# Moving a tenth of the first layer's exponentials from ScalarE to VectorE in a two-attention kernel, with the exponential's bias given as a number

## The chip, the cores and the metric

One core of one Trainium2 chip. The metric is the device time of one launch in microseconds (us). A run is called fast unless it lies over 1.5% above the fastest of the same kernel; only fast runs enter ratios. "Clock" is the mean clock that TensorE was granted over the run, 1.0 being full speed. The engines' names in the profile: DVE is VectorE, POOL is GpSimd, ACT is ScalarE, PE is TensorE.

## The reference, cut to what matters

Two attention layers on separate inputs, 2048 tokens, 32 heads of 16 channels, outputs side by side. The first sees all keys, the second only the last 256.

```python
def _A_ref(x, wqkv, wo):                       # D = 512, H = 32, Dh = 16
    q, k, v = split(x @ wqkv)
    scores = jnp.einsum("bhqd,bhkd->bhqk", q, k) * (Dh ** -0.5)
    p = softmax(scores)
    return (p @ v) @ wo
# _B_ref: the same, with scores masked to 0 <= query - key < 256
# result: concatenate([_A_ref(...), _B_ref(...)], axis=-1)
```

Almost all work is the exponential: 2048 x 2048 x 32 for the first layer, some 12% of that for the second.

## The kernel before

A **job** is one head, 128 keys and 512 queries. Four jobs (four heads) make a group, sixteen groups a unit of the first layer; there are 32 such units, and 32 short ones of the windowed layer strewn between them. Three jobs share a **slot**: a score tile of three PSUM banks, of which there are two, and one exponential over 3 x 512 columns.

```python
def scores(self, slot):                        # TensorE, two slots ahead
    sps = self.ps.tile([P, SLOT, 512], FP32, name="sps", tag="sps", bufs=2)
    for b, jb in enumerate(slot["jobs"]):
        r = slice(32 * jb.j, 32 * jb.j + KR)   # 32 of the 128 rows
        if b == 0 and self.filled < 2:         # "idle fill": a 128-row product,
            self.nc.tensor.matmul(sps[:, 0, 0:WARM], ...)   # overwritten at once
        ...
        self.nc.tensor.matmul(sps[:, b, ...], lhsT=kT[r, ...], rhs=qT[r, ...], ...)

def exps(self, slot):                          # ScalarE
    nc.scalar.activation(out=pT[:, b:e, :n], in_=sps[:, b:e, :n], func=ACT.Exp, scale=SCALE)
    ...                                        # masks of the windowed layer:
    # diagonal blocks: product with a 0/1 tile on VectorE; the others: a select on GpSimd

def values(self, upto):                        # TensorE, into the one bank "op"
    ...                                        # four products of 32 columns, side by side
```

The program's PSUM tiles are six banks of scores, one bank "op" for values, one bank "ms" for all else (projections, and so on), which VectorE empties. The projections and the output products go in between as `steps`, at most one or two a slot; `self.filled` counts those of the slot before. In each loop TensorE gets: the scores of two slots ahead, the values of an earlier slot, then the steps.

## Time and profile before

| | before |
|---|---|
| time | 1166.54 us at the prediction; 1167.79 with the run beside the change |
| ScalarE busy | 1098.6 us, 94% |
| VectorE, GpSimd busy | 298.2 and 119.0 us |
| TensorE clock | 0.939 |
| full exponentials (1536 columns) | 782, one every 1.33 us when nothing is waited for |

The prediction below shows the lines. In a line of a group, the first numbers are busy time and the mean length of one instruction; then come the engine's idle time just before them and what ended it. The row of tenths named PEclk, one figure per fortieth of the span, is near 9 almost throughout, and falls to 6 and 7 near the end, where the kernel has few steps to place.

### The profile page before, as it was taken

The numbers are of one execution on the slowest core, as the hardware profiler recorded it, in microseconds if no ns is written. First come the engines' busy times: TensorE is split into PE (matmuls) and PEld (weight loads), VectorE is DVE, ScalarE is ACT, GpSimd is POOL, SyncE is SP. The second block draws the span as 40 slices with busy tenths as digits, with TensorE's granted clock in tenths as the row PEclk, the third lists the DMA queues.
The fourth block names the chain that finished last, engine by engine and source line by source line (L and its number), as shares of the span: only waits on it lengthen the run. The fifth ranks groups of instructions, "written<-read, shape, count | busy, mean of one in ns | idle before, by whom it ended". The sixth has DMA issues, their size and how long they took to land.

```text
span 1169.9 us, 17451 instructions
## 1 busy us (share of the span) xinstructions
PE 926.1 (79%) x6844; PEld 270.6 (23%) x6944; DVE 298.2 (25%) x674; ACT 1098.6 (94%) x841; POOL 119.0 (10%) x316
## 2 busy tenths in 40 slices
PE   6788888878878887777778787787777887788893
PEld 3222222222222222222222222222222222222221
DVE  3442121132123222222322232224223132320101
ACT  3789999998999999999999999999999999999992
POOL 4000000010001001011200121102112011210100
PEclk9999899998999898999999999999999999976777
DMA  6022421221222112211220221124012112210101
GB/s 207 10 77 75 99 83 41 61 63 52 65 78 76 45 42 65 70 47 61 83 66 32 75 76 54 39 68 118 26 48 65 65 65 69 66 43 18 57 19 55
DMA packets 72810, 73.87 MB, mean 63 GB/s; under 512 B 22688, under 2 KB 55832, under 8 KB 72728
## 3 DMA queue, kind: packets, MB, share of 16 engines
q1 hardware_dynamic: 69656, 68.83, 19.3%
q10 hardware_dynamic: 2432, 1.84, 0.5%
q0 software_dynamic: 640, 2.10, 0.5%
q8 instruction: 54, 0.88, 0.3%
q14 instruction: 28, 0.23, 0.1%
HBM read 39.06 MB, written 31.58 MB: 60 GB/s over the span
## 4 chain that ended last, share of the span: by engine, by line
ACT 62%; PE 21%; issue 11%; DVE 3%; DMA 1%; POOL 0%; ACTq 0%; another core or an unknown queue 0%; SPq 0%; DVEq 0%; POOLq 0%
ACT pT L480 61%; PE sps L462 6%; PE sps L457 6%; PE ms L202 4%; PE op L514 4%; DVE va L285 1%; DVE osb L533 1%; PE ms L591 0%; DMA den<-od 0%; DVE pT L491 0%; DMA rb<-rd 0%; PE sps L358 0%; ACT xT L610 0%; DVE padmax L394 0%; DVE kTa L392 0%
## 5 line engine op out<-in xcount | busy, mean ns | idle before, releaser
L480 ACT ACTIVATE pT<-sps 128x1536 bf16<-128x1536 f32 (+4 forms) x827 | 1088.4, 1566 | 32.8 <-PE sps L462 31.1
L457 PE MATMUL sps<-qTa,kTa 128*128 128x512 bf16 x659 | 261.0, 396 | 159.2 <-ACT pT L480 152.9
L462 PE MATMUL sps<-qTa,kTa 32*128 32x512 bf16 x2048 | 286.5, 404 | 1.5 <-ACT pT L480 1.5
L514 PE MATMUL op<-pT,va 128*32 128x512 bf16 x2048 | 216.4, 412 | 0.5 <-DVE osb L533 0.3
L493 POOL TENSOR_SCALAR_AFFINE_SELECT pT<-pT 128x256 bf16<-128x256 bf16 (+2 forms) x224 | 102.5, 475 | 967.7 <-issue 556.6
L462 PEld LDWEIGHTS <-kTa 32*128 32x128 bf16 x2048 | 68.2, 91 | 395.3 <-issue 395.3
L491 DVE TENSOR_TENSOR pT<-pT,mlo 128x256 bf16<-128x256 bf16 (+2 forms) x256 | 74.9, 334 | 136.3 <-ACT pT L480 134.9
L457 PEld LDWEIGHTS <-kTa 128*128 128x128 bf16 x659 | 64.3, 98 | 144.4 <-issue 124.4
L514 PEld LDWEIGHTS <-va 128*32 128x32 bf16 x2048 | 53.7, 94 | 125.5 <-issue 125.0
L457 PE MATMUL sps<-qTb,kTb 128*128 128x512 bf16 x128 | 51.2, 400 | 34.8 <-ACT pT L480 32.7
L533 DVE COPY osb<-op 128x512 f32<-128x512 f32 x64 | 44.2, 691 | 85.2 <-PE op L514 84.9
L462 PE MATMUL sps<-qTb,kTb 32*128 32x384 bf16 (+2 forms) x704 | 58.4, 289 | 0.0
L220 DVE CAST kst<-ms 128x512 bf16<-128x512 f32 x28 | 19.4, 691 | 141.4 <-PE ms L202 141.4
L343 DVE CAST ob<-ms 128x512 bf16<-128x512 f32 x28 | 19.4, 691 | 131.8 <-PE ms L202 131.8
L301 DVE CAST qs<-ms 128x512 bf16<-128x512 f32 x31 | 21.4, 690 | 115.1 <-PE ms L202 115.1
L514 PE MATMUL op<-pT,vb 128*32 128x384 bf16 (+2 forms) x704 | 36.6, 290 | 0.9 <-DVE osb L533 0.7
L202 PE MATMUL ms<-xT,wq 128*128 128x512 bf16 x91 | 32.2, 408 | 4.7 <-issue 4.3
L462 PEld LDWEIGHTS <-kTb 32*128 32x128 bf16 x704 | 16.9, 93 | 79.7 <-issue 79.7
L202 PE MATMUL ms<-wv,xT 128*128 128x512 bf16 x103 | 32.0, 398 | 4.2 <-issue 1.6
L202 PE MATMUL ms<-xT,wk 128*128 128x512 bf16 x89 | 30.9, 413 | 3.5 <-issue 2.7
L285 DVE CAST vb<-ms 128x512 bf16<-128x512 f32 x16 | 11.1, 692 | 84.5 <-PE ms L202 84.5
L312 DVE CAST gs<-ms 8x512 bf16<-8x512 f32 x31 | 21.0, 677 | 20.0 <-PE ms L310 20.0
(80 smaller groups left out, 274.8 us busy)
## 6 DMA issues: line engine op xcount, KB each, us to landing
od<-osb SPq DMA_DIRECT2D x64, 256.0 KB
oc<-od SPq DMA_DIRECT2D x32, 256.0 KB
rb<-rd SPq DMA_DIRECT2D x32, 256.0 KB
kTb<-kd SPq DMA_DIRECT2D x16, 256.0 KB
qTb<-qd SPq DMA_DIRECT2D x16, 256.0 KB
qd<-qs SPq DMA_DIRECT2D x31, 128.0 KB
qTa<-qd SPq DMA_DIRECT2D x15, 256.0 KB
out_dram<-ob SPq DMA_DIRECT2D x30, 128.0 KB
```

The source lines that it names most:

```text
L202: self.nc.tensor.matmul(bank, lhsT=lhs(c), rhs=rhs(c), start=(c == 0), stop=(c == NC - 1))
L220: copy(out=kst[:], in_=bank)
L285: copy(out=v3[:, :, 1:VP], in_=bank.rearrange("p (h d) -> p h d", d=DH))
L301: copy(out=qs[:], in_=bank)
L312: self.nc.vector.tensor_copy(out=gs[:], in_=b[0:8, :])
L457: self.nc.tensor.matmul(sps[:, 0, 0:WARM], lhsT=kT[:, gg, k0:k0 + P], rhs=qT[:, gg, 0:WARM], start=True, stop=True)
L462: self.nc.tensor.matmul(sps[:, b, o:o + q1 - q0], lhsT=kT[r, gg, k0:k0 + P], rhs=qT[r, gg, q0:q1], start=True, stop=True, tile_position=(3 ...
L480: nc.scalar.activation(out=pT[:, b:e, :n], in_=sps[:, b:e, :n], func=ACT.Exp, scale=SCALE)
L491: nc.vector.tensor_mul(out=v, in0=v, in1=self.mlo[:, 0:e - b, :])
L493: nc.gpsimd.affine_select(v, v, pattern=[[0, e - b], [-1, P]], compare_op=ALU.is_ge, fill=0.0, base=-1, channel_multiplier=1)
L514: self.nc.tensor.matmul(op[32 * jb.j:32 * jb.j + 32, q0:q1], lhsT=self.v[jb.inst, kt][:, h * VP:h * VP + 32], rhs=slot["pT"][:, b, o:o + q ...
L533: nc.vector.tensor_copy(out=osb[:], in_=self.op[i, p, g][:])
```

## The change

Intent: ScalarE is busy for 94% of the span and VectorE for 25%, so VectorE takes a tenth of the first layer's exponentials (196 of 2048 jobs). The scores of a moved job are scaled so that their fp32 value, written as a 16-bit whole number, has the bits of a bf16 power of two; a cubic in the low half corrects it. To have one kind of scores for both engines, the queries are scaled by log2(e) and 128 and carry an offset, which ScalarE takes off with a bias. Masks leave VectorE, and several buffers shrink to make room. The diff is cut: masked values are also used one slot later, and the start-up has other filler products; e1_no_moved, below, keeps all of it but the moved jobs.

```diff
-QRING = (3, 4)
-KRING_B = 10
-VRING_B = 12
+QRING = (3, 3)
+KRING_B = 8
+VRING_B = 10
+FIRST_D = 4                # units 0 to 3 move nothing
+PACE_D = (2, 2, 2, 1)      # groups moved per unit, in turn
 # exps
             nc.scalar.activation(out=pT[:, b:e, :n], in_=sps[:, b:e, :n], func=ACT.Exp,
-                                 scale=SCALE)
+                                 scale=LN2 / 128, bias=-127 * LN2)
-                if kind == "d":
-                    nc.vector.tensor_mul(out=v, in0=v, in1=self.mlo[:, 0:e - b, :])
-                else:
-                    nc.gpsimd.affine_select(...)
+                nc.gpsimd.affine_select(...)          # both kinds
 # new: one step per moved job
+    def poly_ok(self, key):
+        return key[:2] + (key[2] // 2,) in self.qT and len(self.dq) < 4
+    def poly_steps(self, group):
+        def step(jb):
+            b = self.bank()                           # the one bank "ms"
+            nc.tensor.matmul(b[:], lhsT=kT[r, ...], rhs=..., ...)
+            nc.vector.tensor_copy(out=y[:, half, :], in_=b[:])
+            if half == 0:
+                return
+            # first, second: dh = f(low 16 bits of y); third: pD = dh * c + y
+            # each a scalar_tensor_tensor on 128 x 1024
+            self.dq += [first, second, third]
 # end of each slot
+            for _ in range(min(2, len(self.dq))):
+                self.dq.pop(0)()
```

## The prediction

> **What bounds the kernel now.** I read, in this order, the busy shares, the chain of waits, the groups by shape, and the timeline of one steady stretch. The busy shares name the engine:

> ```profile
> PE 926.1 (79%) x6844; PEld 270.6 (23%) x6944; DVE 298.2 (25%) x674; ACT 1098.6 (94%) x841; POOL 119.0 (10%) x316
> ...
> PEclk9999899998999898999999999999999999976777
> ```
> ScalarE is busy for 94% of the span; VectorE and GpSimd for 25% and 10%; the granted TensorE clock (PEclk, tenths) is near full until the last eighth. Whoever takes exponentials away from ScalarE shortens the span, as long as something else does not become the pace. The chain of waits, by engine, agrees:

> ```profile
> ACT 62%; PE 21%; issue 11%; DVE 3%; DMA 1%; POOL 0%; ACTq 0%; another core or an unknown queue 0%; SPq 0%; DVEq 0%; POOLq 0%
> ```
> ScalarE carries most of it; the TensorE part is the hand-over of scores, since PSUM holds two score tiles of three banks. The groups by shape (busy us, mean ns, then idle time before them) give the sizes:

> ```profile
> L480 ACT ACTIVATE pT<-sps 128x1536 bf16<-128x1536 f32 x782 | 1058.6, 1608 | 30.4 <-PE sps L462 28.9 <-DVE pT L491 1.0
> ...
> L457 PE MATMUL sps<-qTa,kTa 128*128 128x512 bf16 x659 | 261.0, 396 | 159.2 <-ACT pT L480 152.9
> ...
> L533 DVE COPY osb<-op 128x512 f32<-128x512 f32 x64 | 44.2, 691 | 85.2 <-PE op L514 84.9
> L493 POOL TENSOR_SCALAR_AFFINE_SELECT pT<-pT 128x384 bf16<-128x384 bf16 x70 | 43.2, 625 | 265.7 <-issue 177.9 <-ACT pT L480 79.7 <-POOL pT L493 4.4
> ...
> L493 POOL TENSOR_SCALAR_AFFINE_SELECT pT<-pT 128x256 bf16<-128x256 bf16 x84 | 38.2, 468 | 455.2 <-ACT pT L480 271.6 <-issue 178.2 <-POOL pT L493 4.6
> ...
> L491 DVE TENSOR_TENSOR pT<-pT,mlo 128x384 bf16<-128x384 bf16 x86 | 30.9, 381 | 77.1 <-ACT pT L480 76.3 <-POOL pT L493 0.7
> ...
> L493 POOL TENSOR_SCALAR_AFFINE_SELECT pT<-pT 128x128 bf16<-128x128 bf16 x70 | 22.9, 334 | 246.8 <-issue 200.5 <-ACT pT L480 40.4 <-POOL pT L493 4.7
> ...
> L559 DVE TENSOR_TENSOR oTb<-oc,rb 128x512 bf16<-128x512 f32 x16 | 11.0, 685 | 21.0 <-DMA rb<-rd 21.0
> ```
> Of the exponentials 782 are full slots (three jobs of 512 columns); they waited only 30.4 us in all. The 659 products of L457 are extra products that the program puts in when little other work was placed; they are idle fill, so TensorE's 79% overstates it. The mean of 1608 ns contains time queued behind the one before, so the price of a slot comes from the timeline, five in a row:

> ```profile
> start us, us, engine line op out<-in xcount [idle before <-releaser]
> 599.72 6.83 ACT L480 ACTIVATE pT<-sps 128x1536 bf16<-128x1536 f32 x5
> ```
> Five end 6.83 us after the first starts. With the last one's own length of about 1.5 us left out, four starts take 5.33 us: **1.33 us a slot**. (Busy time over count, 1058.6/782, gives 1.35 with small waits in it.) By the same timeline TensorE places one idle-fill product, three scores and four value products in about 0.96 us of such a slot: it can be late by a few tenths of a us plus the one buffered slot before ScalarE notices, about 1.3 us in all.

> [...]
> - [...] The first eight full exponentials of this trace, before a queue forms, have a mean of 1459 ns (the groups of the stretch from 26 to 40 us). [...] the built instructions of both kernels show a plain number there. That part of the title buys nothing by itself; it only undoes the offset in the new scores.
> - [...] the trace's 128x512 fp32 product (L559, shown above) has a mean of 685. [...]
> - [...] the 128x384 selects have a mean of 625 ns, while single ones with no two-input VectorE work beside them have 516 to 520 (read instruction by instruction).

> **The change part by part.**
> 1. *Removed from ScalarE.* 28 of the 32 units of the full attention give up 2, 2, 2, 1 of their 16 key groups in turn: 49 groups of 4 jobs, 196 jobs of 2432. The new program's instruction order has 716 full exponentials in place of 782, with two or three more of the small shapes. 66 x 1.33 = 87.8 us, less about 1 us for the small ones: **87 us off the bounding engine.**
> 2. *Added to VectorE.* Each pair of jobs needs two PSUM evacuations of 128x512 fp32 (691 ns, the row of L533) and three fused operations on 1024 fp32 columns (1.22 us): 1.38 + 3.66 = 5.04 us; 98 pairs: 494 us. The 256 mask products leave (30.9 + 26.6 + 22.5 by shape; their union is 74.9 us). 298 - 75 + 494 = 717 us. Over some 1125 us that is 64%: on average it fits. The scaled evacuation of the queries keeps the shape of the cast it replaces, so it costs the same.
> 3. *Added to GpSimd.* The 256 masks become selects: 86 x 0.625 + 84 x 0.468 + 86 x 0.334 = 122 us; 119 + 122 = 241 us before stretching. Masked values are now used three slots after their exponential, about 4 us.
> 4. *TensorE.* The number of score and value products stays. The 196 moved scores stand alone, go through the single one-bank tile "ms", and cost a few tenths each in slack. Idle fill falls by 70.
> 5. *Ends.* Start-up and epilogue keep their work: the first four units have no such jobs, and the last epilogue is unchanged. ScalarE's first exponential starts at 26.7 us and its last ends at 1147.9; the 782 full ones at 1.33 and 29 us of smaller ones make 1069 us of those 1121. The 52 us lost there I leave as they are.

> **What it gives back.** The average hides bursts. In the program's order, 33 of the 49 groups place their four evacuations within at most six successive slots, 5.4 on average = 7.2 us of ScalarE's time. VectorE then owes 2 x 5.04 = 10.1 us plus its other work, (298-75)/746 slots = 0.3 us a slot, 1.6: 11.7 us. Operations without a dependence overlap by some 80 ns (a copy of 691 ns lets the next start after 608), which takes off about 0.6. So a fast group overruns by 11.1 - 7.2 = 3.9 us. TensorE works in order, and "ms" cannot be rewritten until VectorE, also in order, has evacuated it: a late evacuation stops the next scores, then ScalarE. One group's overrun is absorbed: the three fused operations of its last pair (3.7 us) stand ahead of no evacuation that is waited for, and TensorE may be 1.3 us late. The 21 units with two groups overrun by 7.8, absorb 5.0 and lose 2.8 us; with the fast share, 33/49: 21 x 0.67 x 2.8 = **40 us given back**. Masks that come late [...]: my guess is another 6 us over 32 window units. Net 87 - 40 - 6 = 41: 1166.5 - 41 = **1126 us** (rounded up).

> **The rivals.**
> - *Full gain.* VectorE stays hidden, the bursts are smoothed by the two buffered slots, and the time is 1166.5 - 87 = 1080. For it: 64% average load, three buffers for the fp32 results' outputs and two for the inputs. Against it: one "ms" bank and one "op" bank, both emptied by VectorE.
> - *VectorE becomes the pace.* If the fused operations depend on each other so tightly that none overlap, and output copies (64, from the single "op" bank) stall as well, a two-group unit loses 4 to 5 us: 21 x 4.5 = 95 us, and the time stays at 1160 to 1175. For it: in the densest stretches the order asks for 2 us of VectorE per slot of 1.33. Against it: the pace 2, 2, 2, 1 looks chosen by measuring, and at a dead loss a lighter pace would have been chosen. That is a judgement, not a measurement.
> - *GpSimd becomes the wait.* One window unit now has 16 selects, 6.5 us in 5.3 us of slots plus 4 us of grace. Stretched by half they would just miss: 2 us for each of 24 later units, 50 us, and 1150 in all with VectorE's part smaller.

> **Range and chances.** The gain of 87 is sure to within 2 us; what is given back may be 10 to 80. That puts 8 in 10 between 1094 and 1158. Faster by over 2% means below 1143, a give-back under 64: I give it 0.68; within 2% 0.27; slower 0.05, since it needs over 110 us of new waits.

> **What would show it.** ScalarE's count 716 and 1.33 us a slot show step 1; an unchanged 1450 to 1460 ns for an unqueued exponential shows that the immediate is neutral. VectorE busy near 717 us and fused operations near 1.22 us show step 2; GpSimd at 240 to 280 us shows step 3. The give-back should show as ScalarE waiting for scores by some 75 to 100 us in place of 31, behind TensorE waiting on "ms" for the evacuation of the fp32 scores. I am wrong if the fused operations take far less or more than 1.22 us, if TensorE's wait falls on GpSimd's masks instead, or if the granted clock, 0.94 now, changes enough to pace the scores.

Measured beside it: its 1.22 us for a fused operation was not shown by any trace then, as no row of the kernel before has such an operation; in the changed kernel the medians are 1.224 to 1.225 us. The plain number that it names is the exponential's bias; eight exponentials without a queue have a mean of 1459 ns before and 1451 after. That TensorE waits behind VectorE for "ms", which it takes from the program's order, shows in the changed kernel as 38.4 us in 37 waits. The scaled evacuation of the queries takes 690 ns (L311), as the cast before it (L301). The 6 us for late masks stay a guess.

## The result, and the profile after

**Slower: 1246.24 us** (1245.47 to 1249.84, four runs) against 1167.79. The ratio is 1.065, with a 95% interval of 1.059 to 1.071. Ratios here are the mean time of one kernel's fast runs over that of the other's in the same rounds, so not quite the ratio of the medians quoted.

The page of the changed kernel, busy shares, the row of the granted clock in tenths per fortieth of the span, and the chain of waits by engine:

```profile
PE 1057.6 (85%) x6818; PEld 274.1 (22%) x6890; DVE 721.5 (58%) x909; ACT 1033.8 (83%) x776; POOL 239.8 (19%) x575
...
PEclk8999876798877978769778697975797679955577
...
PE 39%; ACT 28%; DVE 21%; issue 10%; DMA 1%; POOL 0%; another core or an unknown queue 0%; ACTq 0%; DVEq 0%; POOLq 0%
```
ScalarE's busy time fell by 65 us (it contains some queueing, so it is not the 87 us of its own work), but its share fell from 94% to 83%: it waits. The clock row that read 9 almost throughout now reads 5 to 8 in most places; the mean went from 0.939 to 0.793. TensorE leads the chain and VectorE has 21% of it, from 3%.

The groups by shape, for the exponentials and for the three fused operations:

```profile
L493 ACT ACTIVATE pT<-sps 128x1536 bf16<-128x1536 f32 x716 | 992.6, 1484 | 170.5 <-PE sps L473 110.2 <-PE op L580 54.2 <-POOL pT L504 3.1
...
L544 DVE SCALAR_TENSOR_TENSOR dh<-dy 128x1024 f32<-128x1024 uint16 x98 | 128.6, 1312 | 3.4
L548 DVE SCALAR_TENSOR_TENSOR dh<-dy,dh 128x1024 f32<-128x1024 uint16 x98 | 121.4, 1239 | 3.4
L554 DVE SCALAR_TENSOR_TENSOR pD<-dh,dy 128x1024 uint16<-128x1024 f32 x98 | 120.5, 1229 | 1.8
```
All 716 exponentials are there; the idle time before them went from 30.4 to 170.5 us, ended by score products and by value products of TensorE. The fused operations have the predicted length, but for some that were held up in the first of the three.

The longest waits that matter, each with us in total, times, and the longest:

```profile
ACT pT L493 <- PE sps L473: 111.9, 189, 3.3
...
ACT pT L493 <- PE op L580: 54.2, 49, 4.0
...
PE ms L531 <- DVE dy L534: 38.4, 37, 3.5
PE op L580 <- DVE osb L599: 29.0, 18, 3.9
```
TensorE waits for VectorE 38.4 us on "ms" and 29.0 us on "op", some 67 us; ScalarE waits 166 us for TensorE. The rest of its waiting is not for a TensorE that stands waiting for VectorE. Two neighbouring stretches of 50 us (busy time of each engine, then the clock) say how:

```profile
500.00:550.00 50.00, 42.66 (x240) 9.47 (x239) 34.99 (x39) 37.57 (x27) 10.27 (x16) 0.65 0.13 41
550.00:600.00 50.00, 42.87 (x349) 12.59 (x351) 22.83 (x35) 50.00 (x39) 12.21 (x32) 1.00 0.23 65
```
In the stretch at full clock ScalarE never pauses. In the one at 0.65 it works for 37.6 of 50 us, though TensorE is as busy as next door. The timeline of 8 us shows the fall from one state into the other:

```profile
601.86 5.11 POOL L504 TENSOR_SCALAR_AFFINE_SELECT pT<-pT 128x256 bf16<-128x256 bf16 x11
...
603.17 3.64 DVE L544 SCALAR_TENSOR_TENSOR dh<-dy 128x1024 f32<-128x1024 uint16 x1
...
604.49 0.39 PE L473 MATMUL sps<-qTa,kTa 32*128 32x512 bf16 x3
606.85 1.23 DVE L548 SCALAR_TENSOR_TENSOR dh<-dy,dh 128x1024 f32<-128x1024 uint16 x1
607.99 0.68 DVE L599 COPY osb<-op 128x512 f32<-128x512 f32 x1
...
608.73 0.63 PE L580 MATMUL op<-pT,vb 128*32 128x128 bf16 x8 [3.85 <-DVE osb L599]
...
609.47 1.45 ACT L493 ACTIVATE pT<-sps 128x1536 bf16<-128x1536 f32 x1 [4.00 <-PE op L580]
...
610.36 0.61 PE L473 MATMUL sps<-qTa,kTa 32*128 32x512 bf16 x3
```
Read from the top. GpSimd has selects in a row; at 603.17 VectorE starts a fused operation, which lasts 3.64 us in place of 1.22. (One by one: six selects run on for 2.42 us after its start, the fused operation ends 1.22 us after that, and the seventh select takes 1.37 beside it.) Behind it, in order, wait the second fused operation and the evacuation of "op" (607.99). TensorE needs "op" for its next values and stands idle for 3.85 us; ScalarE waits 4.00. When TensorE resumes, each score product takes 0.61 us in place of 0.39, and the exponential after the one at 609.47 starts 2.14 us later.

The trace records the clock as stretches of full or half speed, all of them multiples of 3.41 us long but the last, which the end cuts off. I added them up, and split ScalarE's loss (the time from the first to the last exponential's start, less each one's own unhindered time: 1.330 us for a full slot, 0.903 for 1024 columns, and so on) by the clock in which it fell:

| | at half clock | ScalarE's loss | of it at half clock | full slot, median at half clock |
|---|---|---|---|---|
| before | 145 us | 52 us | 32 us | 1.63 us |
| changed | 518 us | 214 us | 173 us | 1.93 us |

So the 87 us off ScalarE did arrive (exponentials' own time: 1068 to 981 us), and 162 us came back: 141 of them inside stretches at half clock.

### The profile page after: what moved, and what is told of

Its sections match the earlier page's. It is cut to its first block, busy times and chain, and to the rows that moved or that the text cites. A ratio compares the mean times of both kernels' runs of the same rounds, so it can differ in the third digit from the quotient of the medians.

```text
span 1245.1 us, 17681 instructions
## 1 busy us (share of the span) xinstructions
PE 1057.6 (85%) x6818; PEld 274.1 (22%) x6890; DVE 721.5 (58%) x909; ACT 1033.8 (83%) x776; POOL 239.8 (19%) x575
## 3 DMA queue, kind: packets, MB, share of 16 engines
q10 hardware_dynamic: 2432, 1.84, 0.5%
## 4 chain that ended last, share of the span: by engine, by line
PE 39%; ACT 28%; DVE 21%; issue 10%; DMA 1%; POOL 0%; another core or an unknown queue 0%; ACTq 0%; DVEq 0%; POOLq 0%
ACT pT L493 27%; PE sps L468 10%; PE sps L473 10%; PE op L580 9%; DVE dh L544 5%; PE ms L212 5%; DVE dy L534 4%; PE ms L531 4%; DVE dh L548 3%; DVE pD L554 3%; DVE osb L599 2%; DVE va L295 1%; DVE oTb L625 1%; POOL pT L504 0%; DMA kTa<-in_A_x_dram 0%
## 5 line engine op out<-in xcount | busy, mean ns | idle before, releaser
L493 ACT ACTIVATE pT<-sps 128x1536 bf16<-128x1536 f32 (+2 forms) x762 | 1023.6, 1442 | 172.6 <-PE sps L473 111.9
L504 POOL TENSOR_SCALAR_AFFINE_SELECT pT<-pT 128x256 bf16<-128x256 bf16 (+2 forms) x480 | 221.6, 503 | 917.3 <-ACT pT L493 916.8
L468 PE MATMUL sps<-qTa,kTa 128*128 128x512 bf16 x593 | 279.0, 470 | 55.4 <-ACT pT L493 46.0
L473 PE MATMUL sps<-qTa,kTa 32*128 32x512 bf16 x1852 | 299.3, 467 | 1.1 <-ACT pT L493 1.1
L534 DVE COPY dy<-ms 128x512 f32<-128x512 f32 x196 | 134.7, 687 | 128.6 <-PE ms L531 128.0
L531 PE MATMUL ms<-qTa,kTa 32*128 32x512 bf16 x196 | 97.1, 495 | 41.1 <-DVE dy L534 38.4
L544 DVE SCALAR_TENSOR_TENSOR dh<-dy 128x1024 f32<-128x1024 uint16 x98 | 128.6, 1312 | 3.4
L548 DVE SCALAR_TENSOR_TENSOR dh<-dy,dh 128x1024 f32<-128x1024 uint16 x98 | 121.4, 1239 | 3.4
L554 DVE SCALAR_TENSOR_TENSOR pD<-dh,dy 128x1024 uint16<-128x1024 f32 x98 | 120.5, 1229 | 1.8
L311 DVE TENSOR_SCALAR qs<-ms 128x512 bf16<-128x512 f32 x31 | 21.4, 690 | 76.8 <-PE ms L212 66.6
L212 PE MATMUL ms<-xT,wq 128*128 128x512 bf16 x101 | 33.7, 397 | 3.1 <-issue 1.3
```

The costliest lines, as they stand in the source:

```text
L212: self.nc.tensor.matmul(bank, lhsT=lhs(c), rhs=rhs(c), start=(c == 0), stop=(c == NC - 1))
L468: self.nc.tensor.matmul(sps[:, 0, 0:WARM], lhsT=kT[:, gg, k0:k0 + P], rhs=qT[:, gg, 0:WARM], start=True, stop=True)
L473: self.nc.tensor.matmul(sps[:, b, o:o + q1 - q0], lhsT=kT[r, gg, k0:k0 + P], rhs=qT[r, gg, q0:q1], start=True, stop=True, tile_position=(3 ...
L504: nc.gpsimd.affine_select(v, v, pattern=[[0, e - b], [s, P]], compare_op=ALU.is_ge, fill=0.0, base=base, channel_multiplier=-s)
L531: nc.tensor.matmul(b[:], lhsT=kT[r, g % 2, k0:k0 + P], rhs=self.qT[0, p, g // 2][r, g % 2, :], start=True, stop=True, tile_position=(32 * ...
L534: nc.vector.tensor_copy(out=y[:, half, :], in_=b[:])
```

## The experiments

**Theory Q.** VectorE is late in bunches; TensorE, in order, idles behind it; its clock is halved; and at half clock its work no longer fits into ScalarE's slot. **Rivals:** G, GpSimd's masks (or the smaller rings) are the cause. M, the mix on TensorE is: lone products of 32 rows and an idle-fill product in each slot. All runs are three timed rounds and one profiled run against the kernel before; medians in us.

| run | jobs moved | placing | idle fill | time | ratio to before | clock | at half clock, us |
|---|---|---|---|---|---|---|---|
| before | 0 | | 1 | 1168 | 1 | 0.939 | 145 |
| the change | 196 | bunched | 1 | 1246 | 1.065 | 0.793 | 518 |
| e1_no_moved | 0 | | 1 | 1172 | 1.002 | 0.938 | 146 |
| e2_thin_poly (wrong results) | 196 | bunched | 1 | 1132 | 0.966 | 0.878 | 278 |
| e3_masks_vector | 196 | bunched | 1 | 1254 | 1.070 | 0.788 | 533 |
| e4_b_masks_gpsimd | 0 | | 1 | 1170 | 0.999 | 0.938 | 146 |
| e7_half_even | 112 | spread | 1 | 1153 | 0.984 | 0.869 | 306 |
| e8_all_even | 196 | spread | 1 | 1177 to 1204 | none | 0.809 | 462 |
| a_no_fill | 196 | bunched | 0 | 1195 | 1.021 | 0.664 | 805 |
| b_no_fill | 0 | | 0 | 1184 | 1.012 | 0.588 | 979 |
| e9_thin_no_fill (wrong results) | 196 | bunched | 0 | 1105 | 0.945 | 0.674 | 723 |
| e10_b_fill2 | 0 | | 2 | 1150 | 0.984 | 0.991 | 22 |
| e11_half_even_fill2 | 112 | spread | 2 | 1133 | 0.969 | 0.978 | 52 |
| e12_a_fill2 | 196 | bunched | 2 | 1244 | 1.064 | 0.852 | 371 |
| e13_thin_fill2 (wrong results) | 196 | bunched | 2 | 1106 | 0.944 | 0.958 | 95 |
| e14_half_even_no_fill | 112 | spread | 0 | 1155 | 0.987 | 0.643 | 828 |
| e15_all_even_fill2 | 196 | spread | 2 | 1141 | 0.976 | 0.963 | 88 |
| e16_half_bunched_fill2 | 112 | bunched | 2 | 1166 | 0.997 | 0.954 | 108 |
| e17_half_even_room | 112 | spread | 2, none after a moved job | 1131 | 0.967 | 0.975 | 58 |
| e18_thin_room (wrong results) | 196 | bunched | 2, none after a moved job | 1143 | 0.976 | 0.861 | 319 |

Clock and half-clock time are those of the profiled run; those of e7 and e8 fell among the slow runs.

### Which part of the change: e1, e4, e3

e1_no_moved moves no job and keeps all the rest.

```diff
-PACE_D = (2, 2, 2, 1)
+PACE_D = (0,)
```

> The changed program with no job moved (all 2432 on ScalarE); masks on GpSimd, scaled queries, smaller rings and the new bias stay. Theory Q (the fused operations make VectorE late, TensorE then idles for over 1 us and its clock is halved): with no fused operation it is like the kernel before, 1160 to 1180 us, mean granted clock 0.92 to 0.95, ScalarE waiting 30 to 45 us. Rival G (the masks on GpSimd, or the smaller rings, make the waits): 1200 us or more, clock under 0.87.

1172.24 us, ratio 1.002, clock 0.938. Masks on GpSimd, scaled queries, the bias, and the smaller rings together cost nothing that these runs can tell (the interval of the ratio is 0.995 to 1.008).

e4_b_masks_gpsimd is the kernel before with the mask part alone.

```diff
-                if kind == "d":
-                    nc.vector.tensor_mul(out=v, in0=v, in1=self.mlo[:, 0:e - b, :])
-                else:
-                    nc.gpsimd.affine_select(...)
+                nc.gpsimd.affine_select(...)
```

> The kernel before with only the diagonal masks moved to GpSimd (values still used two slots later). Theory Q: within 1% of before, 1160 to 1180 us, since GpSimd's 240 us are off the path when VectorE is lightly loaded. Rival G: 1190 us or more, with TensorE's value products waiting for the selects.

1170.07 us, ratio 0.999. e3_masks_vector goes the other way and gives the changed kernel its mask products back.

```diff
+                if kind == "d":
+                    nc.vector.tensor_mul(out=v, in0=v, in1=<one 128 x 128 tile, repeated>)
+                else:
                     nc.gpsimd.affine_select(...)
```

> The changed kernel with its 256 diagonal masks back on VectorE as products (75 us more there, 122 us less on GpSimd). Theory Q: VectorE has more to do in front of the evacuations, 1245 to 1275 us, clock the same or lower. Rival G (GpSimd's selects block the fused operations, of which three took 2.1 to 3.6 us in place of 1.22, and delay masked values): 1200 us or less.

1253.72 us: no better (7 us more by the medians, but the intervals of the two ratios, 1.065 to 1.075 and 1.059 to 1.071, overlap). G falls as the main cause. The held-up operation of the timeline is real but rare: of the 294 fused operations four took over 2.1 us, each with selects of GpSimd right before and beside it, and all that ran over their 1.23 us come to 11 us together.

### VectorE's work or TensorE's mix: e2

All 196 jobs stay moved; only VectorE's part of them is made thin. Its output is wrong, which doesn't matter for the time.

```diff
-  scalar_tensor_tensor(out=h[:], in0=low, ..., in1=low, ...)        # first
+  scalar_tensor_tensor(out=h[:, 0:64], in0=low[:, 0:64], ..., in1=low[:, 0:64], ...)
   # second likewise
-  scalar_tensor_tensor(out=pD, in0=h, ..., in1=flat, ...)           # third
+  memset(pD as fp32, 0.0)
```

> Wrong results on purpose: all 196 jobs stay moved, each with its score product, its evacuation and its value product, but the first two fused operations work on 64 of 1024 columns and the third is a fill of zeros, so that VectorE has about 2.3 us a pair in place of 5.05 (some 450 us busy in all, from 721). Theory Q: the gaps and the half clock go, 1080 to 1100 us, clock 0.90 or more. Rival M (the mix on TensorE does it: lone 32-row products and one-bank hand-over thin out its work, whatever VectorE costs): 1190 us or more with the clock under 0.85. In between: both.

1131.8 us, clock 0.878, VectorE busy 453.5 us. Between the two: taking 268 of VectorE's 370 us of fused work away is worth 114 us, and some 50 us above the 1080 of the full gain remain, with 278 us still at half clock.

### The idle fill and the clock: b_no_fill, a_no_fill, e9

The idle fill is there to keep TensorE's clock up. Taking it out of either kernel:

```diff
-            if b == 0 and self.filled < 2:
+            if False:
```

> The kernel before without its 787 idle-fill products. If activity sets the clock: mean clock below 0.65 (from 0.94), though no wait for VectorE was added. Time: if three scores and four value products at half clock still fit into a slot of 1.33 us, 1165 to 1200 us; if not, 1220 us or more.

1184.35 us, only 1.2% slower, at a clock of 0.588. The clock row of this run:

```profile
PEclk9995555655555555556566655556555666555566
```
Half speed nearly throughout, with no wait for VectorE added: in this kernel the clock goes with TensorE's products, 0.588 without the fill and 0.939 with it. Yet at half clock a slot of three scores and four values is no longer than ScalarE's (median 1.330 us in these stretches). **Half clock by itself does not lengthen this kernel's typical slot**; half clock plus the idle fill does: with it the median is 1.63 us. It is not free, though: ScalarE's loss is 66 us, 55 of it at half clock, against 52 with one fill and 30 with two (e10, below).

> The changed kernel without the idle-fill products (the 128-row product ahead of a slot's scores, 717 of them). If TensorE's activity sets its clock, the mean clock falls from 0.79 to below 0.65. In time two things oppose: at half clock the fill costs a slot about 0.45 us that ScalarE waits for. If the slow stretches are bound by TensorE's work at half clock, the slot there drops from 1.93 to 1.4 to 1.5 us and the time falls to 1150 to 1200 us in spite of the lower clock. If the stretches are bound by waits for VectorE, the time stays at 1240 us or rises.

1194.57 us, 52 us *faster* than the change at a lower clock still. The slot at half clock has a median of 1.35 us in place of 1.93. In the changed kernel the fill holds the clock at 0.793 in place of 0.664, but it makes the slow stretches slower (by 0.58 us a slot, where 0.45 had been estimated), and that costs more than it saves. The theory needed this part: falling to half clock with the fill in each slot adds to the gap behind VectorE.

> Wrong results on purpose: the thin fused operations and no idle-fill products. With the thin operations alone the time was 1132 us, some 50 above what ScalarE's saved work would give. If those 50 us are TensorE's work at half clock (the idle fill among it), they shrink without the fill: 1090 to 1115 us at a clock below 0.7. If they are VectorE's remaining evacuations, the time stays at 1125 to 1140.

1104.74 us at a clock of 0.674: 27 us less than with the fill, as the first reading said.

### Two fills: e10, e12, e13

```diff
-                self.nc.tensor.matmul(sps[:, 0, 0:WARM], ...)
+                for _ in range(2 - self.filled):
+                    self.nc.tensor.matmul(sps[:, 0, 0:WARM], ...)
```

> The kernel before with two idle-fill products after a slot without other work, one after a slot with one step, none after two. If the clock follows TensorE's activity, the half-clock time falls from 145 us to below 60 and the time by 10 to 30 us, to 1140 to 1160. If more fill delays the scores at full clock (a slot of 0.96 us becomes 1.2 to 1.27 of 1.33), 1170 us or more.

1150.03 us, 1.6% faster than the kernel before, with a clock of 0.991 and 22 us at half clock. The lost time of the old kernel was partly this.

> The changed kernel with the doubled idle fill and nothing else. If gaps of 1 to 4 us behind VectorE halve the clock whatever is done in other slots, it stays near 1240 us or gets worse, as each half-clock slot then carries one more product. If low activity in general is what counts, the clock rises above 0.88 and the time falls below 1200 us.

1244.47 us: no gain, though the clock rose to 0.852. The half-clock time fell from 518 to 371 us, but a slot there now takes 2.06 us, and ScalarE's loss is the same in all: 213 us, with 141 at half clock (from 173) and 72 at full clock (from 41). With VectorE as late as here (67 us of waits on "ms" and "op"), the second fill does not help.

> Wrong results on purpose: thin fused operations and doubled idle fill, so neither of the two suspected causes is there. If they are all of it, the 87 us of ScalarE's work arrive in full against the kernel before with the same fill (1150 us): 1060 to 1085 us, clock 0.95 or more. If something else costs too (the one-bank hand-over, the masks on GpSimd): 1095 us or more.

1105.86 us: **the second branch.** Both causes gone, 43 us are left against e10 less 87 (1063). It is hardly late VectorE: TensorE waits 5.0 us on "ms" and 3.6 on "op" in this run, in place of 36.7 and 30.6. These six runs of bunched jobs make a square (us):

| idle fill | change's fused operations | thin fused operations | the difference |
|---|---|---|---|
| none | 1195 | 1105 | 90 |
| one | 1246 | 1132 | 114 |
| two | 1244 | 1106 | 139 |

The 268 us of fused work cost 90 to 139 us at each of the three fills, and the fill moves the time by 1 to 52 us. All three bunched kernels fall to half clock (805, 518 and 371 us of it); what late VectorE costs at a clock that stays full was not measured.

### Total or bunching: e7, e8, e16, e15, e14

The spread form starts moved jobs only some slots apart and queues one fused operation a slot. e7_half_even has one group a unit (112 jobs) and a distance of three; e8_all_even has all 196, a distance of two, and starts them up to 16 slots ahead.

```diff
-        return ... in self.qT and len(self.dq) < 4
+        return ... in self.qT and len(self.dq) < 3 and self.slot - self.lastD >= 3   # e8: 2
-            for _ in range(min(2, len(self.dq))):
+            for _ in range(min(1, len(self.dq))):
```

> One key group per unit in place of 1.75 (112 jobs moved, 50 us off ScalarE), its score products at least three slots apart, and at most one fused operation queued per slot. Right results. Theory Q (late VectorE, then idle TensorE, then half clock): VectorE is never over one slot behind, the clock stays at 0.90 or more and most of the 50 us arrives: 1115 to 1140 us. Rival M (thin products on TensorE lower the clock by themselves): clock under 0.87 and 1150 us or more.

1152.54 us, ratio 0.984 from three fast runs of 1146.6 to 1157.95, clocks 0.88 to 0.90; one run of 1165.1 counts as slow. A miss for Q: VectorE is hardly late (in the profiled run, the slow one, TensorE waits for its evacuations of "ms" and "op" some 6 us in all), yet the clock is under 0.90 in two of the four runs. Something on TensorE's own side, rival M, has a part in it; with two fills (e11, below) the same jobs take 20 us less.

> All 196 jobs moved as in the change, but started up to 16 slots ahead, at least two slots apart, with at most one fused operation queued per slot. Right results, the same VectorE work of 720 us, spread. Theory Q: the waits shrink by more than half, clock 0.85 to 0.90, 1140 to 1190 us. If it is the total on VectorE and not its bunching: still 1230 us or more.

1177.38, 1196.08, 1203.02 and 1204.34 us: only one counts as fast, so there is no ratio. The clock goes with it: 0.856 in the fastest, 0.809 to 0.825 in the others. No other kernel here spreads as far. It is under the 1245 of the bunched form in all four.

The same comparison with the clock held up by two fills is the sharp one.

> All 196 jobs, evenly spread, doubled idle fill. If the bunching was what made VectorE late, 1110 to 1140 us with the clock over 0.93. If VectorE's total (720 us, of which other evacuations must pass) is too much however it is spread, 1160 us or more.

1141.24 us, a little over the forecast of 1110 to 1140. Against e12_a_fill2 (1244.47) it has the same jobs, the same VectorE work, the same fill: **the placing alone is worth 103 us.** TensorE's two waits for VectorE, in e12_a_fill2 and then here:

```profile
PE ms L532 <- DVE dy L535: 36.7, 32, 3.5
PE op L581 <- DVE osb L600: 30.6, 20, 4.1
```

```profile
PE ms L213 <- DVE dy L537: 10.6, 11, 2.5
...
PE op L583 <- DVE osb L602: 5.6, 10, 1.1
```
With 6.6 us more on "ms" (at L321), 67 us have become 23. ScalarE's loss, counted as above, fell from 213 to 108 us, and all of that at half clock: from 141 to 34 us there, from 72 to 74 at full clock. So what the placing saves is time at half clock (waits for VectorE that fall into such a stretch are counted with it).

> 112 jobs with doubled idle fill, but with the change's own rule of placing them (successive slots, two fused operations a slot). If bunching matters at this total: 1150 to 1170 us against 1133 for the spread form, clock 0.90 to 0.95. If the total alone matters: 1128 to 1138 us.

1165.65 us against 1132.85 for the spread form (e11, below): 33 us for the placing of 112 jobs. Bunching costs time at either total.

> 112 jobs moved, evenly spread, no idle fill. If light TensorE work at half clock fits into ScalarE's slot, as in the kernel before without fill, 1120 to 1140 us at a clock near 0.6; if the moved jobs' lone products push the half-clock slot over 1.33 us, 1145 us or more.

1155.48 us: the second branch. But the typical slot is hardly pushed over ScalarE's: at half clock a full slot has a median of 1.35 us, and 31% of them take over 1.4. ScalarE's loss is 88 us, 75 of it at half clock; that it is the lone products was not tested.

### A better version: e11, e17, and what e18 left open

> 112 jobs moved, evenly spread, with the same doubled idle fill. Theory (late VectorE opens gaps, low activity keeps the clock at half): clock 0.93 or more and 1100 to 1130 us, better than both kernels. If half the clock comes from gaps alone, which more products elsewhere do not close: clock under 0.90 and 1145 us or more.

1132.85 us, right results, 3.1% faster than the kernel before and 9% than the change. Its clock row and its full exponentials:

```profile
PEclk8899999999999999999999999999999899999997
```

```profile
L495 ACT ACTIVATE pT<-sps 128x1536 bf16<-128x1536 f32 x741 | 1008.6, 1503 | 33.7 <-PE sps L475 14.8 <-PE op L583 13.7 <-POOL pT L506 1.2
```
The idle time before exponentials is back at 33.7 us, as before the change, with 41 fewer of them.

The last two runs count a moved job's step as two, so that no idle fill follows it.

```diff
-                self.filled += 1
+                self.filled += 2 if self.cur['name'][0] == 'd' else 1
```

> The best version so far (112 jobs, spread, doubled fill: 1133 us) with the same rule. If TensorE's room is what costs there: 1118 to 1130 us. If the missing fill lowers the clock: 1135 us or more and a clock under 0.96.

1130.59 us, ratio 0.967: the same as e11 within their spread, and the fastest of all with right results.

> Wrong results on purpose: as the thin version with doubled fill, but a lone product counts as two steps, so the slot after it has no idle fill. If TensorE's slots around the lone products are too long (0.96 us with one idle product, some 0.2 for the lone product, 0.3 for the moved values), 1080 to 1095 us. If the cost is elsewhere, or the clock falls again, 1105 us or more.

1142.99 us, clock 0.861: the rule that does no harm to spread jobs costs 37 us when they are bunched. There are fewer fill products (842 in place of 1038, by their weight loads), and the clock falls: ScalarE's loss at half clock rises from 26 to 74 us, while that at full clock drops from 49 to 37. So here less fill loses the clock (0.861 in place of 0.958), and more fill seems to fill the slot; how the 43 us left in e13 divide was not settled.

## Why the prediction was wrong

- **Step 1, ScalarE: right.** 716 full exponentials, 1.331 us a slot at full clock, 87 us off the engine's own work.
- **The immediate: right.** The first eight exponentials have a mean of 1451 ns, from 1459; the change of bias bought nothing.
- **Step 2, VectorE: right.** 721.5 us busy against 717; the fused operations have medians of 1.224 to 1.225 us against 1.22, also the two that read 16-bit whole numbers.
- **Step 3, GpSimd: right.** 239.8 us against 241. As a rival cause it fell (e1, e3, e4).
- **Step 4, TensorE, and step 5, "the 52 us lost there I leave as they are": wrong.** Step 4 gave the moved products "a few tenths each in slack", at full speed. The loss rose from 52 to 214 us, 173 of it at half clock. That the 0.96 us of TensorE's work in a slot hold only at full clock (at half clock a full slot took 1.63 us), and that the lost 52 us were themselves mostly half-clock time (32), stood in the old kernel's trace and was not used.
- **The step that failed: "40 us given back".** Its mechanism is the right beginning: bursts, one bank "ms", one bank "op", TensorE in order. Spreading the same work is worth 103 us (e12 against e15), and thinning VectorE's fused work 90 to 139. Its size was wrong. With the fill as it is, taking 268 of the 370 us of fused work away is worth 114 us (e2), against 40 for all of it; and 162 us came back in all, in place of 46 (40 and the masks' 6). A late evacuation was priced as the same delay to ScalarE, less an allowance. In fact it also opens a gap on TensorE, the clock falls, and the next slots take 1.93 us in place of 1.33: 141 of the 162 us lie in stretches at half clock. The allowance of 1.3 us for a late TensorE is in doubt too: its own terms do not add up to it (0.37 us of slack and one slot of 1.33 are 1.7), and in the one case of the timeline above nothing is absorbed: TensorE stands for 3.85 us and ScalarE for 4.00.
- **What would show it.** ScalarE's waiting for scores was put at 75 to 100 us; it was 111.9, and with 54.2 for value products, which that sentence left out, 166. The text did name a change of the granted clock as a thing that would make it wrong, but gave it no number and no rival.
- **The chance of "slower"** was put at 0.05, "since it needs over 110 us of new waits"; 162 came. The rival that lay nearest, VectorE as the pace with up to 1175 us, was argued down because the pace "looks chosen by measuring", a judgement without a measurement behind it, as the text says.

The best account that these runs allow: VectorE's fused work costs 90 to 139 us, by the square above, and with two fills most of that because it is bunched (103 of 139 us). In the change as it is, 52 us vanish if the fill is left out. The parts overlap, so they do not add up. The rest is put down to TensorE's own mix, rival M, but not shown: with thin operations 1132, 1105 and 1106 us remain where 1080 was to be expected of the old fill, and how that divides between lost clock, full slots and the hand-over through one bank "ms" stays open.

## What to carry to other kernels

Before moving work to an idle engine, count its bursts against the slot, and ask which in-order engine stands behind it and which single buffer joins the two (here TensorE and "op", 3.85 us of waiting behind one late evacuation); then spread the work before trimming it. Do not price a wait on TensorE by its length alone: in the changed kernel it waited some 67 us for VectorE, and ScalarE lost 162 us more than before, 141 of them at half clock. An idle-fill product helped where it held the clock up (1184 to 1168 us in the kernel before, clock 0.588 to 0.939) and cost 52 us where the clock stayed at 0.793 in spite of it. Look at the clock row first when a kernel that should be faster is slower: here its mean fell from 0.939 to 0.793.
